# Gates of rows 512 to 2047 taken from natural rows of x on VectorE and ScalarE, the first 512 rows of x transposed by DMA, no conversions on GpSimd, and a new written-out order

## The chip, the cores and the metric

The kernel runs on one core of a Trainium2 chip. The metric is the device time of one execution in microseconds (us), lower is better. Three runs of the kernel before were timed on the chip; their median is the time before. One more execution was profiled, and the profile and the trace come from that one.

The engines are named as the profile names them: PE is TensorE (matmuls), PEld its weight loads, DVE is VectorE, ACT is ScalarE, POOL is GpSimd, SP is SyncE, which only issues DMAs here.

## What is computed

x has 2048 rows (tokens) of 448 elements in bf16. Two branches read it and a gate per row mixes them:

```python
g = sigmoid((x * gate_w).sum(-1))            # one number per row
# branch a: a diagonal state space layer with 448 complex states
Lam = Lambda_re + 1j*Lambda_im ; dt = exp(log_dt) ; Lam_bar = exp(dt*Lam)
B_bar = ((Lam_bar - 1)/Lam)[:, None] * (B_re + 1j*B_im)
Bu = x @ B_bar.T                              # complex, 2048 x 448
h[t] = Lam_bar * h[t-1] + Bu[t]               # over all 2048 rows
a = 2 * real(h @ (C_re + 1j*C_im).T) + x * Dskip
# branch b: a dense layer with hidden width 1792
b = silu(x @ w1) @ w2
out = g * a + (1 - g) * b
```

## The kernel before

The 2048 rows go in four chunks of 512 rows (`tc` 0 to 3) and sixteen blocks of 128 rows (`tb` 0 to 15, four in each chunk). The contraction over x (448 = 7 x 64) runs on a PE split into two halves of 64 rows: `step` takes two products of 128 x 512 at once, with 8 matmuls in its first half and 6 in its second half (`close`, which is issued after the first half of the next step). These are the matmuls of L599. Forty-two such steps carry the input product of the state space layer (`bu`, seven slots of 128 states, real and imaginary parts) and the first dense product (`f1`, 14 blocks for each chunk). The second dense product (`ffn2`, L703, 14 matmuls for a block of 128 rows) and the readout of the state space layer (`readout`, L731, 7 matmuls for a block) use all 128 rows of the PE.

The recurrence is made real by rotating: `lanes(tc)` multiplies U (the evicted `bu` products, one buffer for all chunks) by cosine and sine tables on DVE (PA, PB, L652), runs seven real scans along the 512 rows (`tensor_tensor_scan`, L665, results Gf in f32), converts Gf to bf16 (Gb; L671 on ACT, or L669 on POOL for the slots that `GP` names: slots 0 and 1 of chunks 1 and 2), and rotates back (L652) into H, which has two buffers. A chunk's last state is carried to the next by a few tiny instructions on POOL (k1, k2, gin). `readout_weights(k)` scales C on ACT (L757, L759) and DVE (L761, L764) into CP; its scale factors sc1, sc2 come from a chain of small POOL instructions (L562 to L583) behind the sines and cosines of L557 to L559. `skip(tc)` multiplies the chunk's natural rows `xnat` in place by Dskip (L713, DVE). `readout(tb)` forms tf = g*x*Dskip + Tb (L721, DVE), then ot = g*(readout) + tf (L735, DVE), and stores ot. Tb is the second dense product times 1-g, evicted by ACT (L707).

The gates: `gates(tc)` multiplies the transposed x by a column of gate_w on PE (L774, 16 matmuls with one output column each), ACT takes the tanh of the four columns out of PSUM (L779), and POOL makes g and g1 = 1-g of it (L780, L781).

x is needed transposed (xT). Rows 0 to 511 are loaded in natural form by the first DMA, transposed by 16 PE transposes (L441) and copied out of PSUM by two DVE (L447) and two ACT (L449) copies. Rows 512 on come by DMA transposes (L370). B is loaded in natural form (into the buffer that later holds Tb) and transposed on PE (L468). Before the first data come, 15 matmuls on a cleared tile run (`idle`, L425), and two more later.

The order: every operation is put into a `Plan` with an engine, a cost in us and a priority. PE executes its operations in the order in which they are listed in the program. Every other engine takes, in the plan's own simulated time, whichever ready operation could start first, the lower priority number first. The order so found is fixed at build time, each engine then executes its list in order, and waits are semaphores. So a cost in the plan changes nothing but the order. PSUM has 8 banks, and the plan assigns them.

Of the kernel before, what the change touches and what calls it, by code (L numbers as in the profile page):

```python
# [46 lines left out]
class Plan:  # L47
# [6 lines left out]
    SWITCH = 0.10  # L54

# [46 lines left out]
    def order(self):  # L102
# [28 lines left out]
        while len(done) < len(ops):  # L131
# [20 lines left out]
            if o.sem is not None:  # L152
                free[o.eng] = t + o.cost
                if o.bytes > 4096:
                    pipe = max(pipe, t + 1.5) + o.bytes / 260e3
                    o.end = pipe + 0.4
                else:
                    o.end = t + 3.4
            else:
                extra = 0.0  # L160
                if o.eng == "pe":
                    extra = self.SWITCH if o.rows != rows else 0.0
                    rows = o.rows
                free[o.eng] = o.end = t + o.cost + extra
# [97 lines left out]
def bass_gated_mix__ssm_conv_s5__dense_activation_silu__prompt_kernel(nc, A_x, A_Lambda_re, A_Lambda_im, A_B_re, A_B_im, A_C_re, A_C_im,  # L262
               A_log_dt, A_Dskip, B_x, B_w1, B_w2, gate_w, out):
    with ExitStack() as ctx:
# [31 lines left out]
        dsk = sb("dsk", [128, D_MOD], BF16)  # L296
        tf = [sb(f"tf{k}", [128, D_MOD], F32) for k in range(2)]
# [57 lines left out]
        def load(q, dst, src, name, nbytes, prio, reads=()):  # L355
            P.add(q, lambda e: e.dma_start(dst, src), list(reads), [name], 0.55 if q == "sp" else 0.3, prio, sem(), nbytes)
# [9 lines left out]
        def load_xt(tc, n, prio, cost, reads=()):  # L366

            rows = slice(tc * CH, (tc + n) * CH)
            for k, (o, c) in enumerate(((slice(0, 3), slice(0, 384)), (slice(3, 4), slice(320, 448)))):
                P.add("sp", lambda e, o=o, c=c: e.dma_start_transpose(xT[:, o, rows], x2[rows, c]), list(reads),  # L370
                      [f"xT{t}{k}" for t in range(tc, tc + n)], cost[k], prio + k, sem(), n * CH * (1100, 500)[k])

        load_x(0, 0)
        load("sp", Bnat[:, 0:3, :], A_B_re[0:384, :].rearrange("(s p) d -> p s d", p=128), "Bn0", 384 * 896, 1)
        load("sp", Bnat[:, 4:7, :], A_B_im[0:384, :].rearrange("(s p) d -> p s d", p=128), "Bn3", 384 * 896, 2)
        load("sp", Bnat[0:64, 3, :], A_B_re[384:448, :], "Bn1", 64 * 896, 3)
        load("sp", Bnat[64:128, 3, :], A_B_im[384:448, :], "Bn2", 64 * 896, 4)
        for h, (c0, c1) in enumerate(((0, 384), (384, 896))):
            w = w1s[:, :, :].rearrange("p b (q f) -> p b q f", q=2)
            for b in range(3):  # L380
                load("sp", w[:, b, :, c0:c1], B_w1[128 * b:128 * b + 128, :].rearrange("p (q f) -> p q f", q=2)[:, :, c0:c1],
                     f"w1{h}{b}", 128 * 4 * (c1 - c0), 5 + h)
            load("sp", w[64:128, 3, :, c0:c1], B_w1[384:448, :].rearrange("p (q f) -> p q f", q=2)[:, :, c0:c1],
                 f"w1{h}3", 64 * 4 * (c1 - c0), 5 + h)
            load("sp", w1s[0:64, 3, c0:c1], B_w1[320:384, c0:c1], f"w1{h}4", 64 * 2 * (c1 - c0), 5 + h)
        load("sp", w2s[:, :, :], B_w2.rearrange("(fb p) d -> p fb d", p=128), "w2", F_FF * 896, 8)
        load_xt(1, 1, 9, (3.0, 5.0))
        def load_ct(k, dst, src, cost, prio):
            P.add("sp", lambda e: e.dma_start_transpose(dst, src), [], [f"Cn{k}"], cost, prio, sem(), 448 * 800)


        load_ct(0, CT[:, 0:3, :], A_C_re[:, 0:384], 2.0, 11)
        load_ct(1, CT[:, 3:6, :], A_C_im[:, 0:384], 2.0, 12)
# [3 lines left out]
        def late_loads():  # L397
            load_xt(2, 2, 16, (6.0, 1.4), ["Gb7a", "Gb7b"])
            load("sp", dsk[:, :],
                 A_Dskip.rearrange("(o n) -> o n", o=1).partition_broadcast(128).rearrange("p o n -> p (o n)"),  # L400
                 "dsk", 128 * 896, 18, ["Gb7b"])
            for tc in range(1, NCH):
                load_x(tc, 18 + tc, ["Gb7b"])
# [11 lines left out]
        ACT(lambda e: e.preload_act_table(AF.Exp), [], ["tbl"], 1.3, 4)  # L415


        DVE(lambda e: e.memset(PB[:, 0, :], 0.0), [], ["PB0"], 0.2, 0)  # L418

        def idle(n):  # L420
# [6 lines left out]
            P.add("pe", mm, ["PB0"], [tk], 0.107 * n)  # L427

        idle(15)


        def x_transposes(h, n):

            tk = Ps()

            def mm(pe):
                for q in range(2):
                    for b in range(2):
                        o = (q * 2 + b) * 128
                        c = XCOL[2 * n + q]  # L440
                        r = pe.transpose(bk16(tk)[:, o:o + 128], xnat[:, 2 * h + b, c:c + 128], ident[:, :])  # L441
                return r
            P.add("pe", mm, ["xn0", "ident"], [tk], 0.24)
            dst = xT[:, 2 * n:2 * n + 2, 256 * h:256 * h + 256]
            src = lambda: bk16(tk)[:, 0:512].rearrange("p (q n) -> p q n", q=2)
            if n == 0:
                DVE(lambda e: e.tensor_copy(dst, src()), [tk], [f"xT00{h}"], 0.42, 0)  # L447
            else:
                ACT(lambda e: e.activation(dst, src(), AF.Copy), [tk], [f"xT01{h}"], act_cost(512), 0)  # L449

        for h in range(2):
            for n in range(2):
                x_transposes(h, n)

        def xr(tc):
            return [f"xT{tc}{k}" for k in (range(2) if tc else ("00", "01", "10", "11"))]

        def b_transposes(slots, reads, h, to_act):
# [11 lines left out]
            P.add("pe", mm, reads + ["ident"], [tk], 0.06 * 2 * n)  # L470
# [10 lines left out]

        prmn = [f"prm{k}" for k in range(4)]
# [9 lines left out]
        b_transposes(B01, ["Bn0"], 0, False)  # L492
        b_transposes(B01, ["Bn0"], 1, True)
        idle(2)
# [59 lines left out]
        DVE(lambda e: e.tensor_single_scalar(ph[:, 4:8], ph[:, 0:4], 512.0, ALU.mult), ["ph"], ["ph5"], 0.2, 12)  # L554
        DVE(nearest(phk[:, 4:8], ph[:, 4:8]), ["ph5"], ["phk5"], 0.2, 12)
        DVE(minus(ph[:, 4:8], ph[:, 4:8], phk[:, 4:8]), ["ph5", "phk5"], ["ph5"], 0.2, 12)
        ACT(lambda e: e.activation(s8[:, :], ph[:, :], AF.Sin, scale=TURN), ["ph", "ph5", "tbl"], ["s8"], 0.25, 12)  # L557
        ACT(lambda e: e.activation(pha[:, :], ph[:, :], AF.Abs), ["ph", "ph5", "tbl"], ["pha"], 0.25, 12)
        ACT(lambda e: e.activation(c8[:, :], pha[:, :], AF.Sin, bias=hpi[:, :], scale=-TURN), ["pha", "hpi", "tbl"], ["c8"], 0.3, 12)  # L559

        def pt(o, a, b, op, r, w):
            POOL(lambda e: e.tensor_tensor(o, a, b, op), r, w, 0.15, 20)  # L562
        nr, ni, m1, m2, inv, a1, a2, a3 = (c[:, :] for c in cw)
        pt(nr, rc[:, :], c8[:, 0:4], ALU.mult, ["rc", "c8"], ["nr"])
        POOL(lambda e: e.tensor_single_scalar(nr, nr, -1.0, ALU.add), ["nr"], ["nr"], 0.15, 20)
# [5 lines left out]
        POOL(lambda e: e.tensor_single_scalar(inv, inv, 2.0, ALU.mult), ["inv"], ["inv"], 0.15, 20)  # L571
# [8 lines left out]
        POOL(lambda e: e.tensor_copy(sc1[:, 0:3], a1[:, 0:3]), ["a1"], ["sc1"], 0.1, 20)  # L580
        pt(sc1[:, 3:4], a1[:, 3:4], sgn[:, :], ALU.mult, ["a1", "sgn", "sc1"], ["sc1"])
        POOL(lambda e: e.tensor_single_scalar(sc1[:, 4:7], a1[:, 0:3], -1.0, ALU.mult), ["a1", "sc1"], ["sc1"], 0.1, 20)
        POOL(lambda e: e.tensor_single_scalar(sc2[:, :], a3, -1.0, ALU.mult), ["a3"], ["sc2"], 0.1, 20)  # L583
        POOL(lambda e: e.tensor_copy(CC[:, 0:4], c8[:, 4:8]), ["c8"], ["CC"], 0.1, 14)
        POOL(lambda e: e.tensor_copy(CC[:, 4:7], c8[:, 4:7]), ["c8", "CC"], ["CC"], 0.1, 14)
        POOL(lambda e: e.tensor_copy(SS[:, 0:3], s8[:, 4:7]), ["s8"], ["SS"], 0.1, 14)
        POOL(lambda e: e.tensor_single_scalar(SS[:, 4:7], s8[:, 4:7], -1.0, ALU.mult), ["s8", "SS"], ["SS"], 0.1, 14)
        pt(SS[:, 3:4], s8[:, 7:8], sgn[:, :], ALU.mult, ["s8", "sgn", "SS"], ["SS"])
        POOL(lambda e: e.tensor_single_scalar(SX[:, :], SS[:, 3:4], -1.0, ALU.mult), ["SS"], ["SX"], 0.1, 14)

        def half_steps(pe, a, b, lo, hi, start):
            for i in range(len(lo)):
                for p0, (w, xc, tk, c0), k in ((0, a, lo[i]), (64, b, hi[i])):
                    r = pe.matmul(bk(tk), w[p0:p0 + 64, k, c0:c0 + 128], xT[p0:p0 + 64, k, xc:xc + CH],  # L599
                                  start=(start and i == 0), stop=(not start and i == 2))  # L600
            return r

        open_pair = []

        def step(ta, tb):

            (wa, xa, ca, ra, ea), (wb, xb, cb, rb, eb) = ta, tb
            a, b = Ps("pair"), Ps("pair")
            begin = lambda pe: half_steps(pe, (wa, xa, a, ca), (wb, xb, b, cb), (0, 1, 2, 3), (0, 1, 2, 3), True)
            end = lambda pe: half_steps(pe, (wb, xb, b, cb), (wa, xa, a, ca), (0, 1, 2), (0, 1, 3), False)  # L610
            reads = ra + rb

            def evict(a, b):
                ea(a)
                eb(b)
            P.add("pe", begin, reads, [a, b], 0.866, rows=64)
            if open_pair:
                close()
            open_pair.append((end, reads, a, b, evict))

        def close():
            end0, reads0, a0, b0, evict0 = open_pair.pop()
            P.add("pe", end0, reads0, [], 0.65, acc=[a0, b0], rows=64)
            evict0(a0, b0)

        GP = ((), (0, 1), (0, 1), ())


        def u_out(s, tk, on_dve=False):
# [274 lines left out]
```

## Time and profile before

| | |
|---|---|
| three timed runs | 143.34, 143.43, 144.09 us; median 143.43 |
| profiled execution, its own time | 143.92 us |
| span of its instructions | 142.0 us, so 1.92 us lie around the span |
| busy: PE, DVE, ACT, POOL | 137.6 (97%), 126.1 (89%), 79.1 (56%), 34.2 (24%) us |
| moved by DMA | 11.44 MB |

Busy time is the time in which an engine has at least one instruction under way. The chain of work is followed back from the last instruction: each step is what released the one behind it. An instruction's duration includes its latency, and neighbours on one engine overlap a little, so the distance from one start to the next is a little less than the duration; sums below are made from starts where that matters.

### The profile page before, as it was taken

How to read it: one execution, taken by the hardware profiler on the slowest of the kernel's cores; microseconds unless marked ns; L12 is line 12 of the kernel's file. 1: busy time of each engine (PE TensorE's matmuls, PEld its weight loads, DVE VectorE, ACT ScalarE, POOL GpSimd, SP SyncE). 2: the span in 40 equal slices, each digit the busy share in tenths (PEclk: the TensorE clock that was granted, in tenths of full speed). 3: DMA queues.
4: the chain of work that ended last, by engine and by line, in shares of the span. 5: the costliest groups of instructions: out<-in, count | busy, mean ns of one | idle time of the engine just before them, and what ended most of it. 6: DMA issues, size and time to landing. Idle time of an engine off the chain costs nothing.

```text
span 142.0 us, 2706 instructions
## 1 busy us (share of the span) xinstructions
PE 137.6 (97%) x1069; PEld 70.6 (50%) x1069; DVE 126.1 (89%) x145; ACT 79.1 (56%) x148; POOL 34.2 (24%) x66
## 2 busy tenths in 40 slices
PE   6989999999999999999999999999999999999993
PEld 4855555544444544444555554444455555555552
DVE  0399999998899299999999999999999999899393
ACT  3386698798965494889811014898721355411100
POOL 7184000089009520443450002542000000000000
PEclk9999999999999999999999999999999999999999
DMA  4989969201947600101000102000001021000113
GB/s 133 331 258 290 314 133 201 33 0 39 239 103 188 229 5 0 37 0 42 2 31 1 41 29 69 18 18 5 0 30 34 0 69 37 31 1 32 32 65 99
DMA packets 21108, 11.44 MB, mean 81 GB/s; under 512 B 11492, under 2 KB 21096, under 8 KB 21096
## 3 DMA queue, kind: packets, MB, share of 16 engines
q1 hardware_dynamic: 21088, 11.27, 30.5%
q8 instruction: 8, 0.13, 0.4%
q14 instruction: 4, 0.03, 0.1%
q10 hardware_dynamic: 8, 0.00, 0.0%
HBM read 6.25 MB, written 1.84 MB: 57 GB/s over the span
## 4 chain that ended last, share of the span: by engine, by line
PE 96%; DVE 1%; ACT 1%; POOL 1%; issue 0%
PE ps L599 45%; PE ps L703 30%; PE ps L731 15%; PE ps L425 2%; PE ps L441 1%; PE ps L774 1%; ACT BT L475 1%; PE ps L468 1%; POOL cw L562 0%; DVE ot L735 0%; PE ps L751 0%; DVE PB L418 0%; POOL gwc L497 0%; DVE pc L495 0%; DVE cw L570 0%
## 5 line engine op out<-in xcount | busy, mean ns | idle before, releaser
L599 PE MATMUL ps<-xT,w1s 64*128 64x512 bf16 x392 | 47.4, 376 | 0.0
L703 PE MATMUL ps<-w2s,aT 128*128 128x448 bf16 x224 | 44.7, 352 | 0.0
L692 ACT ACTIVATE aT<-ps 128x512 bf16<-128x512 f32 x56 | 30.0, 601 | 5.3 <-PE ps L599 5.2
L599 PEld LDWEIGHTS ps<-xT,w1s 64*128 64x128 bf16 x392 | 21.0, 94 | 22.7 <-issue 0.7
L703 PEld LDWEIGHTS ps<-w2s,aT 128*128 128x128 bf16 x224 | 21.7, 98 | 20.3 <-issue 0.4
L665 DVE TENSOR_TENSOR_SCAN Gf<-rc,gin,PA 128x512 f32<-128x512 f32 x21 | 26.8, 1322 | 0.0
L599 PE MATMUL ps<-xT,BT 64*128 64x512 bf16 x196 | 25.9, 376 | 0.7 <-DVE ph L511 0.6
L707 ACT ACTIVATE Tb<-ps,g 128x448 bf16<-128x448 f32 x16 | 10.1, 633 | 28.0 <-PE ps L703 21.4
L731 PE MATMUL ps<-CP,H 128*128 128x448 bf16 (+1 forms) x119 | 23.2, 341 | 0.0
L671 ACT ACTIVATE Gb<-Gf 128x512 bf16<-128x512 f32 x24 | 14.7, 630 | 8.4 <-DVE Gf L665 8.3
L599 PEld LDWEIGHTS ps<-xT,BT 64*128 64x128 bf16 x196 | 10.7, 94 | 12.1 <-DVE phk L508 0.8
L731 PEld LDWEIGHTS ps<-CP,H 128*128 128x128 bf16 x119 | 11.5, 98 | 9.8 <-issue 0.4
L633 ACT ACTIVATE U<-ps 128x512 bf16<-128x512 f32 x24 | 13.3, 592 | 2.2 <-PE ps L599 2.2
L735 DVE SCALAR_TENSOR_TENSOR ot<-ps,g,tf 128x448 bf16<-128x448 f32 (+1 forms) x17 | 11.1, 650 | 3.2 <-issue 2.2
L669 POOL CAST Gb<-Gf 128x512 bf16<-128x512 f32 x4 | 6.1, 1518 | 23.0 <-DVE Gf L665 23.0
L721 DVE SCALAR_TENSOR_TENSOR tf<-xnat,g,Tb 128x448 f32<-128x448 bf16 x16 | 10.6, 674 | 0.1
L652 DVE TENSOR_TENSOR PB<-Gb,SIN 128x1536 bf16<-128x1536 bf16 (+1 forms) x8 | 8.6, 1087 | 1.2 <-ACT Gb L671 1.1
L652 DVE TENSOR_TENSOR PB<-U,SIN 128x2048 bf16<-128x2048 bf16 (+1 forms) x8 | 8.6, 1080 | 0.0
L652 DVE TENSOR_TENSOR PA<-U,COS 128x3584 bf16<-128x3584 bf16 x4 | 8.1, 2020 | 0.2
L652 DVE TENSOR_TENSOR PA<-PA,PB 128x3584 bf16<-128x3584 bf16 x4 | 8.1, 2018 | 0.0
L652 DVE TENSOR_TENSOR H<-PA,PB 128x3584 bf16<-128x3584 bf16 x4 | 8.1, 2014 | 0.0
L652 DVE TENSOR_TENSOR PA<-Gb,COS 128x3584 bf16<-128x3584 bf16 x4 | 8.1, 2014 | 0.0
(97 smaller groups left out, 100.5 us busy)
## 6 DMA issues: line engine op xcount, KB each, us to landing
xnat<-in_A_x_dram SPq DMA_DIRECT2D x4, 448.0 KB, 6.1
out_dram<-ot SPq DMA_DIRECT2D x15, 112.0 KB, 1.7
w2s<-in_B_w_dram SPq DMA_DIRECT2D x1, 1568.0 KB, 9.3
w1s<-in_B_w_dram SPq DMA_DIRECT2D x3, 256.0 KB, 4.6
w1s<-in_B_w_dram SPq DMA_DIRECT2D x3, 192.0 KB, 4.3
Gb<-Gb SPq DMA_DIRECT2D x8, 64.0 KB, 1.9
U<-U SPq DMA_DIRECT2D x6, 64.0 KB, 2.0
Tb<-in_A_B_re_dram SPq DMA_DIRECT2D x1, 336.0 KB, 3.7
```

Of the source, the lines that this page charges most:

```text
L599: r = pe.matmul(bk(tk), w[p0:p0 + 64, k, c0:c0 + 128], xT[p0:p0 + 64, k, xc:xc + CH], start=(start and i == 0), stop=(not start and i == 2))
L633: ACT(lambda e: e.activation(U[:, s, :], bk(tk), AF.Copy), [tk], [f"U{s}"], act_cost(512), 4)
L652: return DVE(lambda e: e.tensor_tensor(o, a, b, op), r, w, dve_cost(n, 2), prio)
L665: DVE(lambda e, s=s, b=b, init=init: e.tensor_tensor_scan(Gf[:, s, :], rc[:, b:b + 1].to_broadcast([128, CH]), PA[:, s, :], init, ALU.mult ...
L669: POOL(lambda e, s=s: e.tensor_copy(Gb[:, s, :], Gf[:, s, :]), [f"Gf{s}"], [f"Gb{s}"], 0.75, 8)
L671: ACT(lambda e, s=s: e.activation(Gb[:, s, :], Gf[:, s, :], AF.Copy), [f"Gf{s}"], [f"Gb{s}"], act_cost(512), 4)
L692: ACT(lambda e: e.activation(aT[tc % 2][:, fb, :], bk(tk), AF.Silu), [tk, "tbl"], [f"aT{tc % 2}_{fb}"], act_cost(512), 3)
L703: r = pe.matmul(bk(tk)[:, 0:D_MOD], aT[tc % 2][:, fb, o:o + 128], w2s[:, fb, :], start=(fb == 0), stop=(fb == NFB - 1))
L707: ACT(lambda e, tk=tk: e.activation(Tb[:, tb, :], bk(tk)[:, 0:D_MOD], AF.Copy, scale=g1[:, tb:tb + 1]), [tk, f"g1_{tc}"], [f"Tb{tb}"] + [f ...
L721: DVE(lambda e: e.scalar_tensor_tensor(tf[tb % 2][:, :], xnat[:, tb, :], g[:, tb:tb + 1], Tb[:, tb, :], ALU.mult, ALU.add), [f"xn{tc}", f" ...
L731: r = pe.matmul(bk(tk)[:, 0:n], Ht[:, s, o:o + 128], CP[:, s, c], start=(s == 0), stop=(s == NSLOT - 1))
L735: DVE(lambda e, tk=tk, c=c, n=n: e.scalar_tensor_tensor(ot[tb % 3][:, c], bk(tk)[:, 0:n], g[:, tb:tb + 1], tf[tb % 2][:, c], ALU.mult, ALU ...
```

## The change

- Gates of chunks 1 to 3 come from natural rows: `gates(tc)` calls the new `row_gates(tc)` for `tc` above 0. DVE multiplies two blocks of rows (128 x 896) by gate_w, which a new DMA broadcasts to all partitions (gwb); the product is f32 (xg, one buffer for two blocks). ACT copies each block of xg onto itself and sums it along the row into one column (lg). The tanh reads lg. Chunk 0 keeps the PE form, now called `sum_gates`.
- x of rows 0 to 511 comes by two DMA transposes, first on SP's queue. The 16 PE transposes and their four copies go. The natural rows of chunk 0, which `skip` and `readout` need, are loaded with those of the others, after chunk 0's scans.
- The first part of B (slots 0 and 1 and no longer slot 2 with them) is loaded first on ACT's queue, ahead of the four small parameter loads; its transposes come directly after 12 (was 15) matmuls on zeros, both copies of them are on DVE, then 4 more matmuls on zeros, the parameters' transposes, and the first step.
- w1 is loaded in 8 DMAs (was 10), cut at the same column.
- `GP` is empty: all conversions of Gf are ACT's.
- The 512-row sines and cosines (L554 to L559) get priority 1 or 2 (was 12), and with them the POOL chain behind them can run early. Several costs and priorities in the plan change.
- The order on PE is written anew. `ffn2` blocks and steps of three chunks are mixed more finely; the input products of chunk 1 come before the second dense product of chunk 0, the last of them (`bu(1,3)`) after three blocks of it.

The core of the diff (the plan's other costs and the moved functions `half_steps` to `swapped` are left out):

```diff
-        load_x(0, 0)
-        load("sp", Bnat[:, 0:3, :], A_B_re[0:384, :]..., "Bn0", 384 * 896, 1)
+        load("act", Bnat[:, 0:2, :], A_B_re[0:256, :]..., "Bn0", 256 * 896, -1)
+        load_xt(0, 1, 0, (1.45, 0.7))
         load("sp", Bnat[:, 4:7, :], A_B_im[0:384, :]..., "Bn3", 384 * 896, 2)
+        load("sp", Bnat[:, 2, :], A_B_re[256:384, :], "Bn4", 128 * 896, 3)
...
+            load_xt(2, 2, 16, (4.5, 1.4), ["Gb7a", "Gb7b"])
+            for k, (dst, src, name) in enumerate(((gwb, gate_w, "gwb"), (dsk, A_Dskip, "dsk"))):
+                load("sp", dst[:, :], src...partition_broadcast(128)..., name, 128 * 896, 18 + k, ["Gb7b"])
+            for tc in range(NCH):
+                load_x(tc, 20 + (tc - 1) % 4, ["Gb7b"])
...
-        idle(15)
-        for h in range(2):
-            for n in range(2):
-                x_transposes(h, n)
+        idle(12, 0.213)
...
+        b_transposes(B01, ["Bn0"], 0, False)
+        b_transposes(B01, ["Bn0"], 1, False)
+        idle(4, 0.213)
...
         P.add("pe", prm_t, prmn + ["ident"], [tk], 0.3)
-        b_transposes(B01, ["Bn0"], 0, False)
-        b_transposes(B01, ["Bn0"], 1, True)
-        idle(2)
+        step(bu(0, 0), bu(0, 1))
+        b_transposes(B456, ["Bn3"], 0, False)
+        b_transposes(B456, ["Bn3"], 1, True)
...
-        GP = ((), (0, 1), (0, 1), ())
+        GPRIO = 23
+        GP = ((), (), (), ())
...
+        def row_gates(tc):
+            for h in range(2):
+                tb = 4 * tc + 2 * h
+                DVE(lambda e, tb=tb: e.tensor_tensor(xg[:, :, :], xnat[:, tb:tb + 2, :],
+                    gwb[:, None, :].to_broadcast([128, 2, D_MOD]), ALU.mult),
+                    ["gwb", f"xn{tc}"], ["xg0", "xg1"], dve_cost(896), GPRIO)
+                for k in range(2):
+                    ACT(lambda e, tb=tb, k=k: e.activation(xg[:, k, :], xg[:, k, :], AF.Copy,
+                        accum_out=lg[:, tb + k:tb + k + 1]),
+                        [], [f"xg{k}", f"lg{tb + k}"], act_cost(448, 1), 5)
+            return (lambda: lg[:, 4 * tc:4 * tc + 4]), [f"lg{4 * tc + k}" for k in range(4)]
...
         def gates(tc):
+            src, names = row_gates(tc) if tc else sum_gates(tc)
...
+        gates(0)
+        b_transposes(B23, ["Bn4", "Bn1", "Bn2"], 0, False)
+        close()
+        b_transposes(B23, ["Bn4", "Bn1", "Bn2"], 1, True)
         BU(0, (4, 5), (6, 2))
+        F1(0, (0, 8))
         step(bu(0, 3), f1(0, 7))
+        F1(0, (5, 13), (4, 12), (3, 11), (2, 10))
         lanes(0)
+        F1(0, (1, 9))
+        F1(1, (1, 7))
         late_loads()
+        step(f1(0, 6), f1(1, 13))
+        F1(1, (2, 8))
+        BU(1, (0, 1), (6, 2), (4, 5))
         skip(0)
+        F2(0, 1, 2)
+        readout_weights(2)
         close()
+        F1(1, (4, 10))
         readout_weights(0)
         readout_weights(1)
+        step(f1(1, 0), bu(1, 3))
+        close()
+        F1(1, (5, 11), (3, 9))
+        lanes(1)
+        BU(2, (6, 2))
+        F2(3)
+        gates(1)
...
+        C(4)
+        skip(3)
+        F2(8, 13, 9)
+        C(5)
+        F2(14)
+        C(6, 7, 8)
+        F2(11)
+        C(9)
+        F2(12, 10)
+        C(10)
         lanes(3)
         F2(15)
+        C(11, 12, 13, 14, 15)
```

The part left out between `gates(1)` and `C(4)` holds, in this order on PE: 0.4 us of transposes for `readout_weights(3)`, seven steps, `C(0, 1)`, `F2(6, 5)`, three steps with the last `bu` of chunk 2, `C(2, 3)`, `F2(4)`, `F2(7)`, and eleven steps.

## The prediction

> **What bounds the kernel now.** I read the page first, then the chain of waits in order of time, then busy time by stage, then DVE's own timeline. The page's busy lines and the slices of the two busiest engines:
>
> ```profile
> PE 137.6 (97%) x1069; PEld 70.6 (50%) x1069; DVE 126.1 (89%) x145; ACT 79.1 (56%) x148; POOL 34.2 (24%) x66
> ...
> PE   6989999999999999999999999999999999999993
> ...
> DVE  0399999998899299999999999999999999899393
> ```
>
> PE is full from the fourth slice on, DVE nearly so: two engines near their limit. The chain in order of time shows where PE's time lies:
>
> ```profile
> 4.56 1.71 PE ps L441 x16
> ...
> 7.90 1.02 PE ps L599 x8
> ...
> 9.74 0.82 ACT BT L475
> ...
> 10.69 18.95 PE ps L599 x174
> ...
> 44.59 0.48 PE ps L774 x16
> ...
> 68.81 0.89 PE ps L774 x32
> ...
> 132.89 6.65 PE ps L731 x42
> 139.54 0.02 issue
> 139.57 0.45 DVE ot L735
> ```
>
> From 10.69 to 139.54 us PE never waits: 128.85 us of matmuls. Before that lies a start-up of waits, and after it 2.46 us (the last eviction and its store). So only three things move the end: less PE work behind 10.69, an earlier 10.69, or a wait put into the row. The candidate for such a wait is DVE. Busy time by stage (the second column is the stage's length, then PE, PEld, DVE), and two rows of DVE's timeline:
>
> ```profile
> 35.00:49.00 14.00, 14.00 (x134) 6.85 (x131) 9.63 (x10) 9.39 (x19) 6.21 (x19) 1.00 0.76 191
> 49.00:130.10 81.10, 81.10 (x582) 39.41 (x581) 80.13 (x79) 43.91 (x84) 13.78 (x18) 1.00 0.08 24
> ```
>
> ```profile
> 48.98 0.68 DVE L761 SCALAR_TENSOR_TENSOR CP<-Tb,sc,ct 128x448 bf16<-128x448 bf16 x1 [3.07 <-ACT ct L757]
> ...
> 128.07 2.01 DVE L652 TENSOR_TENSOR H<-PA,PB 128x3584 bf16<-128x3584 bf16 x1
> ```
>
> The last H, which the readouts of blocks 12 to 15 need, is ready at 130.1 us. PE starts block 12 at 134.2 (139.54 less four readouts of 1.32 to 1.33). So DVE is 4.1 us ahead at the end, after 5.3 us of idleness between 35 and 130.1 (14.0 - 9.63 + 81.1 - 80.13).
>
> **PE's work.** Chunks 1 to 3 lose their gate matmuls: from the first L774 to the matmul behind, 44.52 to 44.94 and 68.74 to 69.56, so 0.42 + 0.84 = 1.26 us, all on the path. The new order changes between half-array steps and full-array products 9 times in the body instead of 7; a change costs 0.31 or 0.28 us from start to start where neighbours of one kind are 0.20 and 0.19 apart, so about 0.1 each, +0.2. Body: -1.06 us. Everything else on PE is only reordered.
>
> **The start.** Rows to go by: matmuls on zeros are 0.213 us apart and transposes 0.107 until 6.2 us, 0.057 after. First loads land 3.4 us (x, 448 KB) to 3.7 us (B, 336 KB) after issue, B_im 4.7.
>
> ```profile
> 0.73 0.47 SPq L356 DMA_DIRECT2D xnat<-in_A_x_dram  x1
> ...
> 10.71 8.59 SPq L370 DMA_TRANSPOSE xT<-in_A_x_dram  x2
> 19.34 1.33 SPq L389 DMA_TRANSPOSE Tb<-in_A_C_re_dram  x1
> ...
> 34.32 3.08 SPq L370 DMA_TRANSPOSE xT<-in_A_x_dram  x1
> ```
>
> After: 12 zero matmuls end at 1.18 + 12 x 0.213 = 3.74. B's first part (224 KB, ACT's queue, 0.72) lands near 4.1; eight transposes at 0.107 and four zero matmuls at 0.213 take 1.7 us, to 5.9; the parameters, queued behind that load, then 0.25. The transposed x: the row nearest in size is C_re's transpose, 1.33 us to issue and 4.4 to land with little beside it; the 128-column part of chunk 1 landed 3.7 after issue. Issued at 0.73 and 2.2, the two land at 5.1 and 6.0. The other end is chunk 1's large part, 10.1 us to land, but with 1568 KB of w2 ahead of it, or the 1024-row one, 6.6 us; both ends give 5.9 to 7.9 for the first step. I take 6.2, as nothing large is ahead. It was 7.88.
>
> That lead is not kept whole. B_im's load is now third on SP, behind two transposes' issue (1.5 + 0.7): issued near 3.0, landed near 7.7 (was 6.5), so PE waits about 0.5 behind the first half step. Its 12 transposes, the gate matmuls, then B's last rows (issued near 4.8, landing 3.9 to 4.4 later, 9.0), four transposes, the close (0.75 with the change of mode), four more: the next step begins at 10.2. Before it began at 10.69 with that close (0.65) still to come. Lead: 10.69 - 10.2 + 0.65 = 1.1 us; bounds -0.6 and 2.2, from the first step's.
>
> w1's halves are wanted at 13.2 and 16.3; SP issues them from 5.4 to 10.6 and they took 3.5 to 5.0 to land: 12.5 and 15.6, covered by 0.7 us. Chunk 1's transposes go out behind w2 at 11.2 and land near 22.3; wanted at 23.9. If that cover goes, PE stands for the difference.
>
> With no new wait the last matmul ends at 139.54 - 1.06 - 1.1 = 137.4, and block 12 starts at 132.1.
>
> **DVE.** Six products of 128x896 into f32 are added. No row of before does this:
>
> ```profile
> L713 DVE TENSOR_TENSOR xnat<-xnat,dsk 128x1792 bf16<-128x1792 bf16 x4 | 4.3, 1071 | 0.0
> ...
> L511 DVE TENSOR_TENSOR Gf<-Gf 128x512 f32<-128x512 f32 x2 | 1.4, 675 | 0.0
> ```
>
> All in bf16, 1792 elements take 1.0 us from start to start, so 896 take 0.53; all in f32, 512 take 0.60, so 896 take 1.0. I take 1.0, as the result is f32: 6.0 us; the low end is 3.2. [...]
>
> The four POOL conversions go. Beside each, one scan took 1.56 us, where others took 1.25 to 1.28:
>
> ```profile
> L665 DVE TENSOR_TENSOR_SCAN Gf<-rc,gin,PA x21: 1251/1274/1564, 55.4 to 120.5; 128x512 f32<-128x512 f32 x21
> ```
>
> That is 4 x 0.3 = -1.2 us. At the end one eviction and one tf more come ahead of the last H, as PE is then nearer: +1.2. The copies of xT and BT that come and go lie before 8 us, where DVE waits. From 8 to 35 us DVE is busy 26.84 of 27.0 us on the tables and the first lanes, which hang on the parameters and not on x: no lead there. So from 35 us: 9.63 + 80.13 + 6.0 - 1.2 + 1.2 = 95.8 us of work; without any idleness the last H is ready at 130.8, 1.3 us ahead of block 12.
>
> Of the 5.3 us of idleness, the 3.07 in front of L761 should go: it waits for scale factors behind cosines that ACT ran at 41.94, and these now come early. What is left (1.06 for Gb at 35.0, 1.0 scattered) I keep: 2.0. Then H is ready at 132.8 and PE waits 0.7.
>
> **ACT and POOL.** Twelve sums over 448 elements (the nearest, 448 out of SBUF, 0.66; the smallest of its instructions, 0.16, added if the sum is a second one: 0.6 to 0.85 each) and four conversions (0.55): 10 to 13 us on an engine that is idle 37 of the 81 us after 49. Behind a sum that waits for its product, ACT's evictions wait too, and PE for their PSUM banks. I cost this at nothing: a product is 1.0 us, and PE works 1.5 us on one step between two evictions' pairs. If that cover goes, each such place costs up to a product, 1.0 us.
>
> **Sum.** -1.06 - 1.1 + 0.7 = -1.5 us: span 140.5, profiled time 142.4. The profiled run lies 0.5 above the median, so on the median 143.43 - 1.5 = **141.9**. Case A, chance 0.47, its own range 140.9 to 142.8.
>
> **Rivals.** One percent is 1.4 us, and 0.5% (0.7 us) is about the least that a measurement of this kernel can tell from no change.
>
> *DVE becomes the bound (slower).* The place is the wait of block 12 for the last H. It begins at 1.3 us of DVE idleness after 35 us and eats the gain of 2.2 at 3.5. If DVE idles as it did before, 5.3 us, H is ready at 136.1, PE waits 4.0: 143.43 - 2.2 + 4.0 = 145.2. For it: bu(1,3) now follows three blocks of the second dense product, so lanes(1) cannot start before 45 us (was 42.75); xg is one buffer, so a product waits for two sums. Against: weights, skips and products are there to fill. 0.20.
>
> *The first data are late.* x at 7.9 instead of 6.2 gives a lead of -0.6: 143.43 - 1.06 + 0.6, with no wait for H, 143.0. 0.11.
>
> *PE's clock comes later.* Spacing halved 5 us after the first matmul, on an unbroken run of them; now there are gaps for B, parameters and x. [...] 0.06.
>
> *All of it fits:* DVE idle below 1.3, lead 2.2 (or products at 0.53, which free 2.8 us of DVE): 143.43 - 1.06 - 2.2 = 140.2. 0.16.
>
> That the gates still come from PE cannot be: L774's count must fall to 16.
>
> **Numbers.** Faster by over 0.5% (below 142.7): nearly all of A, all of the last, 0.63. Slower (above 144.15): most of the DVE case, some late data, 0.20. Between: 0.17. The range 140.2 to 145.0 leaves out a tenth on each side.
>
> **What would show it.** L774 x16; first L599 near 6.2, an unbroken PE row from about 10.2; twelve new ACT rows near 0.65 and six DVE rows near 1.05; no scan at 1.56; the chain's end with at most 1 us of DVE or ACT before block 12. The forecast is wrong if PE has gaps in the middle, or if the last H ends later than 134.

## The result, and the profile after

The changed kernel takes 142.02 us (median of 6 runs, 141.24 to 144.41; the 144.41 is set aside in the comparison) against 143.57 for the kernel before (6 runs, 143.04 to 144.09). The ratio is 0.9874 with a 95% interval of 0.9843 to 0.9905, that is 1.4 to 2.2 us less. The profiled execution took 142.63 us with a span of 140.8 (before 143.92 and 142.0).

The page of the changed kernel, its busy line and the slices of PE and DVE:

```profile
PE 136.8 (97%) x1004; PEld 67.3 (48%) x1004; DVE 129.7 (92%) x150; ACT 86.2 (61%) x173; POOL 23.2 (16%) x62
...
PE   7899999999999999999999999999999999999992
...
DVE  0359999999899989999999999999999999999993
```

PE has 0.8 us less to do and DVE 3.6 us more. DVE's slices in the second half are now all 9 up to the last one, where before there were an 8 and a 3 among them.

The chain that ended last, in order of time, of the changed kernel (start, length, engine, tile and line; L479 was L599 before, L700 was L703, L728 was L731, L790 was L774):

```profile
5.93 0.21 PE ps L538 x3
6.28 1.82 PE ps L479 x8
8.11 1.39 PE ps L459 x12
9.50 0.40 PE ps L790 x16
...
11.31 22.12 PE ps L479 x204
...
131.65 6.65 PE ps L728 x42
...
```

L790, the gate matmuls, is left with 16, and PE is on the chain from 5.93 us to the last matmul. The readouts at the end follow on without a wait, as before, 1.24 us earlier.

DVE's cover, by the changed kernel's busy time by stage (columns as before) and one row of DVE's timeline:

```profile
35.00:49.00 14.00, 14.00 (x105) 6.45 (x102) 13.42 (x15) 10.92 (x23) 0.71 (x4) 1.00 0.92 209
49.00:131.01 82.01, 82.01 (x567) 39.76 (x566) 81.21 (x80) 50.27 (x106) 7.01 (x14) 1.00 0.08 23
```

```profile
128.99 2.02 DVE L649 TENSOR_TENSOR H<-PA,PB 128x3584 bf16<-128x3584 bf16 x1
```

PE's busy time equals the length of each stage: no gap. The last H is ready at 131.0 us and block 12 starts at 132.97 (138.29 less four readouts of 1.33), so the margin is 2.0 us, where it was 4.1. DVE sits idle for 1.4 us between 35 and 131.0 (14.0 - 13.42 + 82.01 - 81.21), where it was 5.3.

The new work, as the changed kernel's rows for the tile xg list it (least, median and largest duration in ns, first and last start):

```profile
L772 ACT ACTIVATE xg<-xg x12: 560/577/667, 47.8 to 103.0; 128x448 f32<-128x448 f32 x12
L772 ACT ACTIVATION_READ_ACCUMULATOR xg<-xg x12: 185/199/291, 48.3 to 103.4; 128x1 f32 x12
L768 DVE TENSOR_TENSOR xg<-xnat,gwb x6: 1062/1077/1084, 46.7 to 100.1; 128x896 f32<-128x896 bf16 x6
```

A product takes 1.08 us; its neighbours stand 1.0 apart. The sum is a second instruction behind the copy, 0.58 + 0.20 = 0.78 us; as the two overlap, ACT starts its next instruction 0.56 to 0.58 us after the copy where nothing is waited for.

### The profile page after: what moved, and what is told of

Read it like the earlier page. It is cut to its first block, busy times and chain, and to the rows that moved or that the text cites. A ratio compares the mean times of both kernels' runs of the same rounds, so it can differ in the third digit from the quotient of the medians.

```text
span 140.8 us, 2594 instructions
## 1 busy us (share of the span) xinstructions
PE 136.8 (97%) x1004; PEld 67.3 (48%) x1004; DVE 129.7 (92%) x150; ACT 86.2 (61%) x173; POOL 23.2 (16%) x62
## 4 chain that ended last, share of the span: by engine, by line
PE 94%; DMA 2%; ACTq 1%; DVE 0%; issue 0%
PE ps L479 46%; PE ps L700 30%; PE ps L728 15%; DMA prm<-in_gate_w_dram 2%; PE ps L459 1%; ACTq L361 1%; DVE ot L732 0%; PE ps L790 0%; PE ps L748 0%; PE ps L538 0%; PE ps L540 0%
## 5 line engine op out<-in xcount | busy, mean ns | idle before, releaser
L479 PE MATMUL ps<-xT,w1s 64*128 64x512 bf16 x392 | 48.0, 376 | 0.0
L700 PE MATMUL ps<-w2s,aT 128*128 128x448 bf16 x224 | 43.9, 353 | 0.0
L700 PEld LDWEIGHTS ps<-w2s,aT 128*128 128x128 bf16 x224 | 21.7, 98 | 20.9 <-issue 0.4
L479 PEld LDWEIGHTS ps<-xT,w1s 64*128 64x128 bf16 x392 | 20.1, 94 | 23.4 <-issue 0.7
L479 PE MATMUL ps<-xT,BT 64*128 64x512 bf16 x196 | 28.6, 386 | 0.0
L662 DVE TENSOR_TENSOR_SCAN Gf<-rc,gin,PA 128x512 f32<-128x512 f32 x21 | 25.3, 1259 | 0.0
L668 ACT ACTIVATE Gb<-Gf 128x512 bf16<-128x512 f32 x28 | 17.7, 655 | 9.3 <-DVE Gf L662 9.3
L728 PE MATMUL ps<-CP,H 128*128 128x448 bf16 (+1 forms) x119 | 22.5, 342 | 0.0
L704 ACT ACTIVATE Tb<-ps,g 128x448 bf16<-128x448 f32 x16 | 10.2, 636 | 19.7 <-PE ps L700 18.5
L728 PEld LDWEIGHTS ps<-CP,H 128*128 128x128 bf16 x119 | 11.4, 98 | 10.5 <-ACT Gb L668 0.4
L479 PEld LDWEIGHTS ps<-xT,BT 64*128 64x128 bf16 x196 | 10.6, 95 | 11.6 <-issue 0.9
L674 POOL TENSOR_TENSOR k<-Gf,CC 128x7 f32<-128x7 f32 x3 | 2.1, 715 | 56.6 <-DVE Gf L662 56.6
L649 DVE TENSOR_TENSOR PB<-U,SIN 128x1536 bf16<-128x1536 bf16 (+1 forms) x8 | 8.5, 1083 | 0.0
L772 ACT ACTIVATE xg<-xg 128x448 f32<-128x448 f32 x12 | 7.0, 597 | 2.4 <-DVE xg L768 2.3
L662 DVE TENSOR_TENSOR_SCAN Gf<-rc,PA 128x512 f32<-128x512 f32 x7 | 8.2, 1209 | 0.0
```

Source lines behind the costliest of these rows:

```text
L649: return DVE(lambda e: e.tensor_tensor(o, a, b, op), r, w, dve_cost(n, 2), prio)
L662: DVE(lambda e, s=s, b=b, init=init: e.tensor_tensor_scan(Gf[:, s, :], rc[:, b:b + 1].to_broadcast([128, CH]), PA[:, s, :], init, ALU.mult ...
L668: ACT(lambda e, s=s: e.activation(Gb[:, s, :], Gf[:, s, :], AF.Copy), [f"Gf{s}"], [f"Gb{s}"], act_cost(512), 4)
L700: r = pe.matmul(bk(tk)[:, 0:D_MOD], aT[tc % 2][:, fb, o:o + 128], w2s[:, fb, :], start=(fb == 0), stop=(fb == NFB - 1))
L704: ACT(lambda e, tk=tk: e.activation(Tb[:, tb, :], bk(tk)[:, 0:D_MOD], AF.Copy, scale=g1[:, tb:tb + 1]), [tk, f"g1_{tc}"], [f"Tb{tb}"] + [f ...
L728: r = pe.matmul(bk(tk)[:, 0:n], Ht[:, s, o:o + 128], CP[:, s, c], start=(s == 0), stop=(s == NSLOT - 1))
```

## The experiments

All ratios are to the kernel before on the same chip, and 0.01 of them is 1.44 us. The others are held against the control, 0.9887. What the expectations call the third step is the second one: the first `step` is opened by 8 matmuls and closed by 6, and the next 8 open the second.

### The same kernel again, and the clock at the start

**control**: no edit.

> The changed kernel as it is, once more. Theory (the clock's wake drifts): PE's matmuls go from half to full rate at a time that is not tied to the first matmul, so in this profile the change of spacing (0.107 to 0.057 us for transposes, 0.42 to 0.22 for pairs of steps) comes at another time than 9.9 us, and the span follows it: 139.4 if it comes by 6.3, 140.8 if it comes at 9.9. Rival (the wake is fixed by the work): again at 9.9 us, span 140.8 +- 0.1.

Measured: 0.9887 (0.985 to 0.9923), median 141.92, profiled span 140.1 against 140.8. PE's timeline shows where the 0.7 us between two profiles of one kernel lies. The changed kernel:

```profile
6.22 1.89 PE L479 MATMUL ps<-xT,BT 64*128 64x512 bf16 x8
8.04 1.46 PE L459 MATMUL ps<-ident,Tb 128*128 128x128 bf16 x12
...
11.24 1.47 PE L479 MATMUL ps<-xT,BT 64*128 64x512 bf16 x12
```

The control:

```profile
5.86 1.04 PE L479 MATMUL ps<-xT,BT 64*128 64x512 bf16 x8
7.33 0.84 PE L459 MATMUL ps<-ident,Tb 128*128 128x128 bf16 x12 [0.44 <-DMA Tb<-in_A_B_im_dram]
...
9.21 0.38 PE L459 MATMUL ps<-ident,Tb 128*128 128x128 bf16 x4 [0.66 <-DMA Tb<-in_A_B_im_dram]
...
10.61 2.12 PE L479 MATMUL ps<-xT,BT 64*128 64x512 bf16 x18
```

The same 8 matmuls take 1.89 or 1.04 us, the same 12 transposes 1.46 or 0.84: PE ran at half rate until 10.0 us in the one, and in the other it is at full rate from the first step on (5.86). So that time is not tied to the first matmul (at 1.05 and 1.04 us), as the theory said, but the span followed it less far than the theory had it (140.1 and not 139.4).

The second steps are 0.63 us apart. Of this 0.36 is there before the first step: the parameters' transposes start at 5.93 and 5.57. The full rate brings only the other 0.27, because the faster start then waits for B (0.44 and 0.66 us, in brackets), and B's last rows landed at 9.08 us in the control and at 8.48 in the changed kernel. From there to the second step the control takes 1.53 us, so at full rate the changed kernel could have begun it near 10.0 instead of 11.24: by this estimate the late rate cost it 1.2 us.

From the start of the second step to the end of the span the two profiles agree, 129.55 and 129.49 us. All that differs lies before it. Six of the runs below share PE's order up to there and the first loads (pe_gates, double_products, two_more, late_factors, pool_casts, old_order). In all six PE is at full rate from the first step on, and the second begins at 9.81 to 10.28.

**fill**, to keep PE from standing idle before the parameters:

```diff
-        idle(4, 0.213)
+        idle(8, 0.213)
```

> Changed kernel with 8 instead of 4 matmuls on zeros behind B's first transposes: they end near 6.1 us, so PE has no gap between its first matmul and the first step (0.64 us of gap at 5.3 to 5.9 in the changed kernel); the first step starts up to 0.2 later. Theory (an unbroken busy stretch releases the clock): full rate by 8.0 us at the latest, first step and the 12 transposes behind it together 0.7 to 1.4 us shorter whenever they would have run at half rate; time 0.2 to 1.2 us below the control run. Rival (the gap plays no part): 0 to 0.2 us above the control run.

Measured: 0.9854 (0.9821 to 0.9887). Half rate until about 6.7 us, first step 6.58, second step 10.24. It can't be told apart from the control by its interval, and without the longer fill PE came to full rate as early in the control (before 5.9 us), so it isn't shown that the gap plays a part.

**no_zeros**, one matmul on zeros in place of twelve, and one in place of four, at the same planned cost:

```diff
-        idle(12, 0.213)
+        idle(1, 2.556)
...
-        idle(4, 0.213)
+        idle(1, 0.852)
```

> Changed kernel with 1 instead of 12 and 1 instead of 4 matmuls on zeros (their cost in the plan kept, so the order is the same). PE idles from 1.3 to 3.6 us and for longer before the first step. [...] Rival (the zeros play no part): within 0.2 us of the control run.

Measured: 0.9911 (0.9883 to 0.9938). Half rate until 9.9 us and the second step at 11.1, as in the profile of the changed kernel; 0.3 us over the control in the ratio, 0.5 in the medians, where the rival had 0.2 at most. From the second step on the profile takes what the control's takes (129.49 us), so the difference lies in the start, with its late rate. The intervals overlap, and the changed kernel had the same late rate with all its matmuls on zeros: that these bring it forward isn't shown.

### What the gates on VectorE and ScalarE are worth

**pe_gates**: all four chunks take their gates from PE again, and the load of gwb goes.

```diff
-            src, names = row_gates(tc) if tc else sum_gates(tc)
+            src, names = sum_gates(tc)
```

> Changed kernel with the gates of all chunks from PE again (no row products, no sums, no broadcast load of gate_w); the rest is as changed. Theory (PE's own work is the bound): +0.42 us for each of three chunks = 1.26, and +0.2 for the third, which stands between two pieces of half-array work and adds two changes of mode: 1.3 to 1.5 us slower than the control run. Rival A (DVE is the bound of the changed kernel): 6 us of DVE work less, so not slower, up to 2 us faster. Rival B (the gate matmuls hide in gaps): no difference.

Measured: 0.9967 (0.9947 to 0.9987), slower than the control by 1.15 us in the ratio and by 1.45 in the medians (143.37 and 141.92, same chip). The last H comes at 124.6 us, 8.9 ahead of block 12 (133.5): DVE is far from the end again, and what counts is PE's 48 matmuls. The gate matmuls' 1.26 us are on the path, as the prediction had them.

**double_products**: every product is made twice, 6.0 us more on DVE.

```diff
+                for _ in range(2):
                     DVE(lambda e, tb=tb: e.tensor_tensor(xg[:, :, :], xnat[:, tb:tb + 2, :],
```

> Changed kernel with each of the six products made twice (the second writes the same values again): 6.0 us more on DVE. In the changed kernel the last H is ready 1.96 us before block 12 starts, and DVE idles 1.35 us between 35 us and there. Theory (DVE is next to the bound, with about 2 to 3.3 us of room): PE waits 2.7 to 4.0 us for the last H, time 2.7 to 4.0 above the control run. Rival A (DVE already sets the end): +6.0. Rival B (DVE has room for all of it, because its fillers move): within 0.5 us of the control run.

Measured: 1.048 (1.0435 to 1.0525), 8.5 us over the control: over twice what the theory had, and more than rival A's 6.0. The last H comes at 138.25 us, 8.1 later than in the control: 6.0 for the products, the other 2 because more of the outputs' DVE work now ran ahead of it (14 tf and 12 ot, where it was 11 and 10). In PE's timeline of this kernel, the bracket is the idle time before the row; this view ends at 142 us, and the second line, from the chain, has all 35 matmuls behind the wait:

```profile
138.31 3.92 PE L728 MATMUL ps<-CP,H 128*128 128x448 bf16 x10 [6.09 <-DVE H L649]
```

```profile
138.31 8.38 PE ps L728 x35
```

PE waits 6.09 us (8.1 less the margin of 2.0), and then the 35 matmuls take 8.38 us, where the control needs 5.48 for them (132.18 to 137.66): after this gap PE is at half rate again until 143.9 us, fifteen matmuls 0.37 apart instead of 0.19, another 2.9. The mean granted clock is 0.977 in all six runs, 1.0 in the control. 6.1 + 2.9 is the 9.0 by which the two spans differ (149.1 and 140.1).

**two_more**: only chunk 3's two products are made twice, 2.0 us more on DVE.

```diff
+                for _ in range(2 if tc == 3 else 1):
```

> Changed kernel with only the two products of chunk 3 made twice: 2.0 us more on DVE in front of the last H, against a margin of 2.06 us in the control run. Theory (the margin is what the control run shows, and DVE work inside it is free): within 0.4 us of the control run (141.9), the last H within 0.5 us of block 12's start. Rival (queues in order make DVE work cost at once, as ACT's evictions stand behind sums that wait for products): 1 us or more slower, with gaps of PE ahead of block 12.

Measured: 0.9907 (0.9881 to 0.9932), 0.3 us over the control in the ratio, 0.65 in the medians. The last H comes at 131.75 us and block 12 starts at 131.81: the margin of 2.0 is used up, and little is lost. It isn't nothing: the second step of this profile began 0.80 us earlier than the control's, block 12 only 0.37, and DVE's last eviction ends 1.0 us behind PE's last matmul instead of 0.5. From the second step to the end it takes 130.8 us against 129.5. The two runs place the point from which the products decide: about 2 us of DVE work from where the kernel stands, less by what an early start gives PE, and beyond it more than one microsecond for each.

### What makes room for them

**before_row_gates**: the kernel before with row_gates for chunks 1 to 3 and nothing else of the change.

```diff
+            src, names = row_gates(tc) if tc else sum_gates(tc)
```

> The kernel before with one part of the change alone: gates of chunks 1 to 3 from row products on DVE and sums on ACT (gate_w broadcast by one more DMA); order, x, B, POOL conversions and late factors as before. PE loses 1.26 us. Theory (the rest of the change is what makes room on DVE): DVE gets 6.0 us more in front of the last H, of which at most about 4 fall into its idle times (3.07 and 1.06 us), and about 1.2 of readout work is pulled ahead; the last H is ready at 133.3 to 137.3 instead of 130.1 and block 12 could start at 132.9: 0.8 us faster to 3 us slower than before, likeliest 1 us slower. Rival (the gates alone are the gain, DVE has room): 1.26 us faster than before.

Measured: 1.0319 (1.0286 to 1.0351), 4.6 us slower than the kernel before and outside what was expected. PE's last matmul ends at 140.25, but the span is 146.8. The timeline of this kernel, rows of DVE and PE:

```profile
131.83 2.02 DVE L655 TENSOR_TENSOR H<-PA,PB 128x3584 bf16<-128x3584 bf16 x1
...
133.44 6.80 PE L734 MATMUL ps<-CP,H 128*128 128x448 bf16 x42
...
138.52 1.08 DVE L716 TENSOR_TENSOR xnat<-xnat,dsk 128x1792 bf16<-128x1792 bf16 x1
...
143.21 1.40 DVE L738 SCALAR_TENSOR_TENSOR ot<-ps,g,tf 128x448 bf16<-128x448 f32 x3
```

No bracket stands in DVE's rows: it works without a pause on the last chunk's skip and on the outputs, and ends 4.4 us behind PE's last matmul; in the kernel before and the changed one its last eviction ends 0.5 behind. It had stood idle for 6.8 us between 35 us and the last H, 3.1 of them at CP for ACT's ct, while 6 us of products were added. The rival that DVE becomes the bound is real: it is what the row gates do alone. But it isn't where the prediction and this expectation looked: the last H is ready at 133.85 us, 0.9 ahead of block 12, and most of the loss is the outputs behind PE's end. PE itself ends 0.7 us later than before; a new wait of 1.2 us for an eviction by ACT takes nearly all of the 1.26 saved, and the rest isn't resolved.

**late_factors**: the changed kernel, with the six instructions that lead to the scale factors put back to where the kernel before had them.

```diff
-... ["s8"], 0.25, 2)
+... ["s8"], 0.25, 12)
```

> Changed kernel with the old priorities (12) for the sines and cosines behind the carry and the readout weights (L606 to L611), so the scale factors come late again. Theory: DVE idles again in front of the readout weights, 2 to 3 us between 35 and 50 us; the last H comes 2 to 3 us later, against a margin of 2.06 us in the control run: 0 to 1.2 us slower than the control run. Rival (row products and skips fill that time as well): no difference.

Measured: 1.0186 (1.015 to 1.0223), 4.3 us over the control, more than three times the upper end expected. ACT's timeline, then PE's, of this kernel:

```profile
34.19 0.67 ACT L754 ACTIVATE ct<-Tb,sc 128x448 f32<-128x448 bf16 x1 [3.58 <-POOL sc L635]
```

```profile
35.49 2.81 PE L700 MATMUL ps<-w2s,aT 128*128 128x448 bf16 x14 [2.68 <-ACT aT L689]
```

ACT stands 3.58 us at ct for a scale factor; the evictions of the first dense product are queued behind it on ACT, and PE stands 2.68 us for them, 0.35 more for another of them. The expectation had only DVE's 3.07 us at CP in view. The early factors are what lets readout weights stand where the new order has them. All this comes before the first row product (49.5 us), so it is a price of the new order with late factors, not one of the gates. The profile is not the whole: it and one more of the six runs took 145.4 and 145.7 us at a granted clock of 1.0, the other four 146.6 to 146.8 at 0.988. Whether PE ran at half rate behind its gap in those four, no profile shows.

**pool_casts**: the changed kernel with the four conversions back on POOL.

```diff
-        GP = ((), (), (), ())
+        GP = ((), (0, 1), (0, 1), ())
```

> Changed kernel with the four conversions of chunks 1 and 2 back on POOL. Theory: four scans take 1.56 us again, 1.2 us more on DVE, inside the margin of 2.06 us: within 0.3 us of the control run. Rival (DVE sets the end): +1.2.

Measured: 1.0108 (1.0067 to 1.0148), 3.2 us over the control, ten times the bound expected. The scans beside the conversions are back at 1.57 us (the largest in the scans' row, 1284 ns in the changed kernel), but that is the 1.2 us that a DVE with 2 us of margin can bear. What shows of the rest is on the path through ACT. The timeline of this kernel, all engines:

```profile
101.02 0.58 ACT L772 ACTIVATE xg<-xg 128x448 f32<-128x448 f32 x1 [0.74 <-DVE xg L768]
...
104.25 2.07 PE L700 MATMUL ps<-w2s,aT 128*128 128x448 bf16 x10 [1.12 <-ACT aT L689]
```

A sum waits on ACT for its product (0.74), the evictions queued behind the sums come late, and PE stands 1.12 us for them. With 0.40 for another eviction by ACT and 0.23 for one by DVE that is 1.75 us of gaps, of the 2.9 by which PE's work from the second step to the last matmul is longer than in the control. The control's waits show no such wait anywhere. The last H isn't the cause (132.69, block 12 at 134.71). Which of the delayed instructions begins it wasn't taken apart; the planned order also shifts when the conversions change engine.

**old_order**: the changed kernel with PE's order of the kernel before from chunk 0's second slots on.

> Changed kernel with PE's order of before from the second pair of steps on (rows, x, loads, POOL, priorities and costs as changed). PE's own work is the changed kernel's less 0.2 us (two changes of mode fewer). Theory (the new order is needed to keep the products and sums off PE's path): 1.5 to 4 us slower than the control run, that is 143.4 to 146, with gaps of PE at evictions behind sums or at the last H. Rival (early factors and no POOL conversions are enough): within 0.5 us of the control run.

Measured: 0.9851 (0.9823 to 0.9879), the same as the control. The last H comes at 127.69 us, 4.4 ahead of block 12. So the theory that the new order is needed falls: with everything else of the change the old one hides the products as well, with twice the margin. DVE stands idle for 0.4 us between 35 us and the last H here, for 6.8 in before_row_gates.

### The start

**pe_x**: the changed kernel with chunk 0 loaded as natural rows and transposed by 16 matmuls on PE, as before.

```diff
-        load_xt(0, 1, 0, (1.45, 0.7))
+        load_x(0, 0)
...
-        idle(12, 0.213)
+        idle(15, 0.213)
+        # and the four x_transposes of the kernel before
```

> Changed kernel with x of rows 0 to 511 loaded in natural form first and transposed on PE (16 transposes behind 15 matmuls on zeros, 2 zero matmuls behind B's first transposes, its four copies on DVE and ACT); the late load of these rows is left out. Theory: the first step comes at 7.0 to 7.6 us instead of 5.9 to 6.6, but PE is unbroken till then, its clock is up, and B's other rows and w1 arrive no earlier in the changed kernel: the matmul with which the third step begins comes within 0.6 us of where the control run has it, and so does the end. Rival (the transposed loads are worth their lead at the start): 1.0 to 1.5 us slower than the control run.

Measured: 1.0005 (0.9971 to 1.0039), 1.7 us over the control. Its profiled execution took 145.99 against a median of 143.89, so only the order of events is read from it: x landed at 5.4 us, beside the load of B that now goes first on ACT's queue (at 4.1 in the kernel before, where B's loads came behind it), the 16 transposes took 1.89 at half rate, and the first step began at 8.84 (5.86 in the control). Loading x transposed is worth 1.7 us to this kernel, far more than the theory gave it; with intervals of 0.5 us on either side that can't be told from the rival's 1.0 to 1.5. Beside the natural rows B's first part, wanted in the same microseconds, took 4.4 us to land (2.6 in the control), so this is not the old start, and the 1.7 can't be added to what the gates are worth.

**act_loads**: fill, and B's last three small loads on ACT's queue instead of SP's.

> The run with 8 zero matmuls, and besides B's last three small loads on ACT's queue instead of SP's, so that w1, w2 and the later transposes are issued about 1.8 us earlier on SP. Theory (behind the first step PE waits for B's last rows, 0.8 us in the control run, and where it does not, for w1, 0.6 us): the third step begins at 9.6 to 10.1 instead of 10.5 to 10.8, no wait for w1 at 15.4, time 0.3 to 1.0 us below the control run. Rival (loads on two queues share the same engines, so nothing lands earlier): within 0.2 us of the run with 8 zero matmuls (141.7); or the plan's other order on ACT and DVE costs more than that.

Measured: 1.0036 (1.0016 to 1.0057), 2.1 us slower than the control. PE's waits for B still sum to 1.1 us, as in the control, and new ones come: 0.5 us for an eviction by ACT and 0.5 for the last H, which comes at 133.9. The wait for B wasn't shortened by this, and a way to do so was not found.

## Why the prediction was right, step by step

Forecast 141.9, measured 142.02 (141.92 in the control). The mechanism held, PE's row shorter and no wait put into it. That the sum came so close is partly luck: one of its terms was nothing, and another varies by more than a microsecond.

**PE's body**: forecast -1.06 us. From the second step to the last matmul the kernel before took 139.53 - 10.69 - 0.65 (the open close) = 128.2, the changed one 138.29 - 11.24 = 127.05 and the control 137.66 - 10.61 = 127.05. That is -1.14. Step right, and pe_gates shows its cause.

**The lead at the start**: forecast 1.1 us. x landed as put down, at 5.2 and 6.0, and the first step came as forecast, at 6.22 and 5.86 (6.2). But the second began at 11.24 and 10.61 instead of 10.2, so the lead was 10.69 + 0.65 - 11.24 = 0.10 in the one profile and 0.73 in the other, too small by 0.4 to 1.0 us. In the changed kernel's profile the half rate lasted to 10.0 us. In the control, at full rate from the first step, PE waits for B's last rows until 9.21 where 9.0 was forecast, and the two lots of four transposes around the close take 0.32 and 0.33 us from start to start where 0.2 each was put down: 10.61 instead of 10.2. The six other profiles with the same start lie on the other side, at 9.81 to 10.28, a lead of 1.1 to 1.5. So 10.2 is the middle of eight profiles, and what the prediction lacked is the spread of 1.4 us. The rival of a later clock thus happened in the profile compared here, at 1.2 us by the estimate above. Its chance of 0.06 looks low: three of fourteen profiles show half rate to about 10 us, one of these eight among them. In the two profiles of the same code full rate came before 5.9 and at 10.0 us; what sets the time, no run shows.

**The wait for the last H**: forecast +0.7 us, measured none. DVE's work from 35 us was 94.6 instead of 95.8, and its idleness 1.4 instead of 2.0, so H was ready at 131.0, not 132.8. The 1.2 us of work too much is one term: "one eviction and one tf more come ahead of the last H". They don't. DVE's groups between 35 us and the last H, of the kernel before and then of the changed one:

```profile
L721 DVE SCALAR_TENSOR_TENSOR tf<-xnat,g,Tb 128x448 f32<-128x448 bf16 x11 | 7.3, 671 | 0.0
L735 DVE SCALAR_TENSOR_TENSOR ot<-ps,g,tf 128x448 bf16<-128x448 f32 x10 | 6.8, 675 | 0.6 <-PE ps L731 0.6
```

```profile
L718 DVE SCALAR_TENSOR_TENSOR tf<-xnat,g,Tb 128x448 f32<-128x448 bf16 x11 | 7.2, 676 | 0.1
L732 DVE SCALAR_TENSOR_TENSOR ot<-ps,g,tf 128x448 bf16<-128x448 f32 x10 | 6.6, 670 | 0.0
```

Eleven and ten in both. DVE's order is planned, and the plan put none of them ahead. The terms named besides held: six products at 1.0 from start to start, and 1.5 us less in the scans (26.8 to 25.3). Two shifts that the sum doesn't have cancel: one more of chunk 0's scans falls behind 35 us (1.2), and two of the seven DVE products of the readout weights fall in front of it (1.2). The longest scan is 1.28 in the changed kernel's row:

```profile
L662 DVE TENSOR_TENSOR_SCAN Gf<-rc,gin,PA x21: 1247/1255/1284, 56.1 to 122.6; 128x512 f32<-128x512 f32 x21
```

In these two profiles the errors offset each other, which is luck: -1.14 - 0.10 + 0 gives the profile's -1.2 (142.0 to 140.8) and -1.14 - 0.73 the control's -1.9, on either side of the -1.5 put down.

**The idleness of 3.07 us at CP**: forecast to go, and gone; late_factors brings a wait of 3.58 us back, on ACT. **ACT's sums**: 0.78 each, inside 0.6 to 0.85, and at no cost, as no wait of PE for an eviction is left in the control. The price named for a lost cover, up to 1.0 us in each place, is what pool_casts shows in one (1.12).

**The slower rival** (DVE becomes the bound, 145.2) did not come, and the runs place it. The changed kernel stands 2.0 us of DVE work away from it. What keeps it off isn't the new order, as the weights, skips and products "there to fill" suggested: old_order has the margin too, and before_row_gates, with nothing else of the change, loses 4.6 us to the same gates. The place was named wrongly, though. There DVE falls behind in the outputs, after PE, and not at the last H. What makes the room must be in the rest of the change, and the early factors and the conversions off POOL are the likely parts. Neither was taken away by itself under the old order. Under the new one their absence costs 4.3 and 3.2 us, but through ACT, at PE's evictions, and not through DVE's margin.

**What stays open**: which part of the change makes the room on DVE, where in the plan pool_casts' delay begins, and whether old_order or fill (0.9851 and 0.9854) beats the changed kernel (0.9874 and 0.9887); the intervals don't separate them.

## What to carry to other kernels

Work moved from a full engine to one that is 90% busy brought what it took off the full one only together with changes that removed the receiver's idle stretches: count those, find which instruction each waits for, and move that earlier. The same gates cost 4.6 us alone and gained 1.2 to 1.4 with the rest, where DVE's idle time from 35 us on was 6.8 and 1.4 us. When an instruction on an in-order engine can wait, price what is queued behind it and not the wait itself: a scale factor late for one ct cost PE 2.7 us through ACT's evictions. A lead at the start is as long as the latest of all first loads allows, so work it out for the second step and not for the first. Compare two profiles from a point behind the start as well: from the second step on, kernels that differ in the start alone agreed within 0.2 us here, while the second step itself moved by 1.0.

## What the runs showed of the hardware

PE's first matmul started at 1.18 us in the kernel before, at 1.05 in the changed one and at 1.04 in the control and fill; full rate came at 6.2, at 10.0, before 5.9 and at about 6.7, though the changed kernel and the control are the same code. A late one is worth about 1.2 us here, by the estimate made under control. After a PE gap of 6.1 us (double_products) PE ran at half rate for 5.6 us (0.37 us from one readout matmul to the next instead of 0.19). Beside each of the four conversions on POOL one scan took 1.56 us in the kernel before, and with the conversions put back the largest was 1.57 (pool_casts); the other scans of these chunks took 1.25 to 1.28 before, as all of them do in the changed kernel.
